# A capped attention with a mixture of experts behind it: tiles' results evacuated within the next tile, x written by units, weights, tables and orders rearranged, chains of tiles unrolled thrice

## The chip, the cores and the metric

The kernel runs on one core of a Trainium2 chip. The time is the device time in microseconds of one execution. Before the change it is 482.37 us, the median of three runs (481.7 to 484.04).

## The reference

Attention runs over 4 batches, 12 heads, 448 tokens and a head size of 64, and its output is the input of a layer with 8 experts, of which each token takes the best one:

```python
scores = scale * (q @ k.T);  scores = cap * tanh(scores / cap)      # cap = 30
attn = exp(scores - max); attn /= sum + 1e-9;  x = attn @ v         # x: 1792 tokens x 768
logits = normed(x) @ normed(expert_emb).T / tau                     # 8 experts
e = argmax(logits);  gate = softmax(logits)[e]
out = gate * (relu(x @ w1[e]) @ w2[e])                              # w1: 768 x 1024, w2: 1024 x 768
```

How many tokens an expert gets is known only while the kernel runs. All is float32, with products to float32 accuracy.

## The kernel before, in words

**Attention** (attention_bounded, L770 to L1013) goes through 12 units of two pairs of heads, three units to a batch. A unit has 7 steps. An iteration of the loop at L942 issues two steps: scores (TensorE: q times k; ScalarE: tanh, then exp) and, four steps behind, values (TensorE: probabilities times v, summed in PSUM buffers v0 and v1). take (L864) lets VectorE divide a pair's sums into xsb, the rows of x in SBUF. embed_v (L826) fills the columns of the next unit's v that a unit needs besides v; it begins with a memset on GpSimd (POOL) at L830. The order of all instructions is as written: each engine runs its own queue in order and waits on semaphores.

**Routing** runs beside it. When a batch is done, after(b) (L895) puts its steps (choose, ranks, norms, scales, gates, each with a cost in us) on the list route, and writes the batch's x to DRAM with write_rows (L437): two transfers, issued by SP, except that columns beyond the first of the last batch are issued by ScalarE. In each iteration the list is served while the planner's sum behind + cost stays at most OVER = 5.2. Weights of the expert that is to run first are loaded into a ring of three pieces, 14 pieces in all, and split into two float16 parts (split_first, L735); fill is the list of the 28 splits, 16 of which are due in the loop. A product of float32 accuracy is three float16 matmuls: high by high, high by low, low by high. first_table (L589), in batch 2, computes the first tiles' row numbers, gathers 128 rows of x from DRAM by them (gather, L216: POOL, an indirect DMA into xg), then runs scale_x (L224: POOL makes x_tile out of xg) and a second gather. later runs transpose_x (L231: TensorE transposes x_tile; ScalarE and VectorE make its two parts) and scale_x six iterations after.

Behind the loop come the first tile's up products, do_up, with the list ready beside them (fills, count_last, what is left of route), the rest of the first tile (tile0) and a branch, `tc.If(unbounded > 0)`, L1140, that goes to a general attention for large caps and is not taken here.

**Experts.** p numbers the experts in the order in which they run. A tile is 128 tokens of one expert (a half tile 64). tile_body (L629) does, in order: gate times scale and the output rows' numbers on POOL (L643 to L657), up products and relu (L258, L270), down products (L675) of six of eight blocks, transpose_x and scale_x for the tile that follows, the last two blocks, then the evacuation by VectorE and ScalarE (L707, L708), the scatter to out (L716) and the gather for a later tile (L721), both on POOL. hooks are put between the blocks: number n before the n-th of 12 up steps and 8 down steps. todo holds the next expert's weight splits (split1, split2), each of which issues the load of the expert after next (load1, load2, through SP). wide_tile (L1384) is the first tile of experts 1 to 4; it carries 32 extra rows (along) with it, which along_gather, along_scale and along_transpose (L1360 to L1375) fetch, scale and transpose once.

Tile 0b (L1536) follows the first tile, with hooks1 (L1301): order (the experts' order), start_loads (SP loads seven registers, then issues expert 1's loads), the last gates, fill_table (all later tiles' row numbers), positions, start_loads2 (w2 of expert 1), along_gather, load_ends (each engine loads how many tiles each expert has). Then chain(p) (L1551) runs an expert's tiles, nested:

```python
with ExitStack() as es:
    for n in range(1, UNROLL):
        es.enter_context(tc.If(code > 2 * n + 1, label=f"more{p}_{n}"))
        full_tile(p, base + n, (), FIRST, {0: [...]})
    es.enter_context(tc.If(code > 2 * UNROLL + 1, label=f"more{p}_{UNROLL}"))
    with tc.For_i(UNROLL, code >> 1, 1) as n:
        full_tile(p, base + n)
```

With this data three full tiles run for p = 0 behind tile 0b, four tiles (one of them wide) for p = 1, three for p = 2, one each for p = 3 and 4, and a half tile for p = 5. More experts (p = 6 and 7, or a second tile of p = 5) run in a branch, "more", that is not taken; expert 6's weights are loaded ahead of it. L1562 is the line of the exits of the nested branches.

## Time and profile before

| | us |
|---|---|
| median of 3 runs | 482.37 (481.7 to 484.04) |
| profiled execution: its time | 480.64 |
| its span | 478.9 |
| busy in the span: PE (TensorE matmul) | 436.3 |
| VectorE (DVE), ScalarE (ACT), GpSimd (POOL) | 273.2, 267.5, 129.0 |
| moved by DMA | 88.21 MB, 184 GB/s on average |

The span is what the profiler records of one execution; the device time of the same execution is 1.7 us more. Attention takes about the first 178 us, the first two tiles until 227, the other tiles until 468; from there to the end no matmul runs. In the rows below, a wait is an engine's idle time and the instruction or transfer that ended it; "issue" is idle time for which the profile shows no cause; a Q behind an engine's name is its instruction queue (sequencer). The granted clock is TensorE's, in parts of 2.4 GHz.

### The profile page before, as it was taken

Reading aid. Unit: us, or ns where it says so; the run is one execution under the profiler, and the core shown is the slowest. Engines: PE = TensorE matmul, PEld = TensorE weight load, DVE = VectorE, ACT = ScalarE, POOL = GpSimd, SP = SyncE. Lnnn points to the kernel's source line nnn. Section 1 sums busy time; section 2 is a strip of 40 time slices with the busy share of each in tenths; the row PEclk is TensorE's granted clock in tenths of the full one; section 3 lists DMA queues with packets and bytes.
Section 4 is the critical chain, followed back from the end, with each engine's and each line's share of the span. In section 5 each row is a group of like instructions: output and inputs, shape, how many; then the busy total and the mean of one; then the engine's idle time right before and its main releaser. Section 6 shows DMA issues by size and latency. Waiting matters only on the chain. (4 is left out here: it accounts for less than half of the span.)

```text
span 478.9 us, 16552 instructions
## 1 busy us (share of the span) xinstructions
PE 436.3 (91%) x7001; PEld 352.6 (74%) x7002; DVE 273.2 (57%) x714; ACT 267.5 (56%) x292; POOL 129.0 (27%) x229
## 2 busy tenths in 40 slices
PE   7999989999996999597969999999999999999771
PEld 3788878888884987394848868878868978869560
DVE  5265577688999589575831139421239321788610
ACT  3999989998999594423720238110248111849200
POOL 5000000000113020213452339322336521573231
PEclk9999999999999899888989999999999999999977
DMA  6844187484288216159972209622219612498940
GB/s 205 298 161 162 54 280 258 156 281 174 78 332 279 73 54 212 58 169 405 403 275 73 71 23 333 236 71 72 71 37 355 250 40 71 135 383 279 380 110 8
DMA packets 29756, 88.21 MB, mean 184 GB/s; under 512 B 6957, under 2 KB 7241, under 8 KB 29650
## 3 DMA queue, kind: packets, MB, share of 16 engines
q1 hardware_dynamic: 26050, 73.31, 42.4%
q0 software_dynamic: 2816, 13.49, 8.7%
q8 instruction: 62, 1.02, 0.9%
q14 instruction: 44, 0.36, 0.2%
q10 hardware_dynamic: 784, 0.03, 0.1%
HBM read 75.10 MB, written 12.31 MB: 183 GB/s over the span
## 5 line engine op out<-in xcount | busy, mean ns | idle before, releaser
L857 PEld LDWEIGHTS v<-vb,prob 128*64 128x64 f32 (+1 forms) x2688 | 80.8, 137 | 21.7 <-issue 15.9
L857 PE MATMUL v<-vb,prob 128*64 128x73 f32 (+1 forms) x2688 | 88.2, 230 | 6.0 <-POOL vb L830 4.0
L258 PEld LDWEIGHTS <-h 128*128 128x128 f16 x1056 | 81.7, 101 | 8.9 <-issue 4.2
L258 PE MATMUL h<-xh,h 128*128 128x128 f16 (+1 forms) x480 | 81.2, 222 | 6.8 <-DMA w2r<-in_moe_w_dram 3.5
L818 ACT ACTIVATE prob<-s,icap 128x896 f32<-128x896 f32 x84 | 80.1, 998 | 12.7 <-PE s L808 11.5
L258 PE MATMUL h<-xl,h 128*128 128x128 f16 (+1 forms) x480 | 81.1, 222 | 1.9 <-issue 1.9
L258 PE MATMUL h<-xh,l 128*128 128x128 f16 (+1 forms) x480 | 81.1, 222 | 0.0
L822 ACT ACTIVATE prob<-prob,cap_b 128x1792 f32<-128x1792 f32 (+1 forms) x47 | 76.8, 1633 | 1.5
L258 PEld LDWEIGHTS <-l 128*128 128x128 f16 x528 | 53.1, 101 | 2.0 <-issue 2.0
L675 PEld LDWEIGHTS <-hh 128*128 128x128 f16 (+1 forms) x352 | 33.3, 101 | 23.2 <-ACT hh L270 3.2
L225 POOL TENSOR_TENSOR x_tile<-xg 128x768 f32<-128x768 f32 x16 | 23.4, 1465 | 97.1 <-PE xt L236 83.6
L270 ACT ACTIVATE hh<-h 128x512 f16<-128x512 f32 (+1 forms) x20 | 11.5, 576 | 67.1 <-PE h L258 62.9
L271 DVE SCALAR_TENSOR_TENSOR hl<-h,hh 128x512 f16<-128x512 f32 (+1 forms) x20 | 13.2, 662 | 62.5 <-ACT hh L270 62.5
L239 ACT CAST xh<-xt 128x384 f16<-128x384 f32 x30 | 12.9, 481 | 56.2 <-PE xt L236 48.6
L1423 PE MATMUL h<-xh,h 128*128 128x160 f16 x192 | 39.9, 233 | 3.4 <-ACTq L1562 3.4
L249 DVE SCALAR_TENSOR_TENSOR l<-w1r,by_pos,h 128x1024 f16<-128x1024 f32 x30 | 36.9, 1281 | 8.2 <-ACT h L248 8.0
L1423 PE MATMUL h<-xh,l 128*128 128x160 f16 x192 | 39.9, 233 | 0.0
L1423 PE MATMUL h<-xl,h 128*128 128x160 f16 x192 | 39.9, 233 | 0.0
L240 DVE TENSOR_TENSOR xl<-xt,xh 128x384 f16<-128x384 f32 x30 | 15.3, 551 | 42.1 <-ACT xh L239 42.1
L675 PE MATMUL y<-h,hl 128*128 128x384 f16 (+1 forms) x160 | 38.9, 334 | 0.0
L675 PE MATMUL y<-l,hh 128*128 128x384 f16 (+1 forms) x160 | 38.8, 333 | 0.0
L675 PE MATMUL y<-h,hh 128*128 128x384 f16 (+1 forms) x160 | 38.6, 331 | 0.0
(292 smaller groups left out, 845.2 us busy)
## 6 DMA issues: line engine op xcount, KB each, us to landing
w1r<-in_moe_w_dram SPq DMA_DIRECT2D x36, 512.0 KB, 6.3
w2r<-in_moe_w_dram SPq DMA_DIRECT2D x24, 768.0 KB, 9.5
qkb<-in_qk_pairs_dram SPq DMA_DIRECT2D x11, 896.0 KB
vb<-in_v_pairs_dram SPq DMA_DIRECT2D x12, 511.0 KB, 7.9
vt<-in_vt_pairs_dram SPq DMA_DIRECT2D x12, 448.0 KB, 6.9
x_dram<-xsb SPq DMA_DIRECT2D x4, 1296.0 KB
ring<-in_moe_w_dram SPq DMA_DIRECT2D x6, 512.0 KB
ring<-in_moe_w_dram SPq DMA_DIRECT2D x8, 384.0 KB
```

Source lines behind the costliest of these rows:

```text
L225: nc.gpsimd.tensor_tensor(x_tile.rearrange("p (h d) -> p h d", d=DH), heads(xg[:, :SCALE]), xg[:, SCALE : SCALE + 1].unsqueeze(2).to_broad ...
L239: nc.scalar.copy(hi, t)
L240: nc.vector.tensor_tensor(lo, t, hi, op=ALU.subtract)
L249: nc.vector.scalar_tensor_tensor(out=lo, in0=raw, scalar=scale, in1=hi, op0=ALU.mult, op1=ALU.subtract, accum_out=acc)
L258: nc.tensor.matmul(hp[:, f, :W], l[j][:, c], x[:, j, :W], start=j == 0 and f == 0 and n == 0, stop=j == DC - 1 and f == 3 and n == 2, skip ...
L270: nc.scalar.activation(b, a, AF.Relu)
L271: nc.vector.scalar_tensor_tensor(out=c, in0=a, scalar=0.0, in1=b, op0=ALU.max, op1=ALU.subtract, accum_out=acc[:, h : h + 1])
L675: nc.tensor.matmul(y, hidden[h][l][:, c, o : o + k], w2p[p % 2][w][f // 2][:, f % 2, m * C : (m + 1) * C], start=f == 0 and n == 0, stop=f ...
L818: nc.scalar.activation(o, sp[:, :, :S], AF.Tanh, scale=icap)
L822: nc.scalar.activation(o, o, AF.Exp, scale=cap_b)
L857: nc.tensor.matmul(psum_v[2 * i + n][h * DH : (h + 1) * DH, m * VW : (m + 1) * VW], pt[rows, s, c : c + DH], vb[rows, k, s, :], start=m == ...
L1423: nc.tensor.matmul(o, w1p[p % 2][l][j][:, c], x[:, j, :], start=j == 0 and f == fs[0] and m == 0, stop=j == DC - 1 and f == fs[-1] and m == 2,
```

## The change

- The two PSUM buffers of the attention's sums become `held`, for the whole kernel. A full or wide tile leaves its result there. hold notes its gate and rows before transpose_x; release, at the start of the next tile, evacuates and scatters. The gather of a tile no longer stands behind its scatter.
- write_rows is called after each unit, for that unit's columns, in place of once per batch.
- first_table only gathers; scale_x and the second gather come three iterations later (first_scale), transpose_x and scale_x behind that. The list route is served to the loop's end; what is left of it, token_rows of the last batch and order come behind the fills, before the first tile's rest.
- Three of the 14 pieces of the first expert's weights go into buffers of q and k (ring_qk) within the last unit.
- Expert 1's w1 loads come behind the first register load. fill_table, positions and start_loads2 move from hook 11 to 9; the copy that start_loads2 waits for moves to POOL, behind a scale_x. along_scale and along_transpose move from hooks 2 and 17 to 12 and 20.
- Expert 6's weights (LATE) are loaded in the "more" branch alone.
- UNROLL is 3.

```diff
-UNROLL = 4
+LATE = WIDE.stop + 1
+UNROLL = 3
...
+    ps_o = ctx.enter_context(tc.tile_pool(name="ps_o", bufs=1, space=PSUM))
+    held = [ps_o.tile([P, 512], F32, tag=f"v{n}", name=f"v{n}") for n in range(2)]
+    held_g = small.tile([P, 1], F32, tag="held_g", name="held_g")
+    held_i = small.tile([P, 1], I32, tag="held_i", name="held_i")
+    def hold(idx, unscaled):
+        nc.gpsimd.tensor_tensor(held_g, gate, unscaled, op=ALU.mult)
+        nc.gpsimd.tensor_copy(held_i, idx)
+    def release():
+        yo = tile_of("o", 0)
+        nc.vector.tensor_scalar(yo[:, :384], held[0][:, :384], held_g, None, op0=ALU.mult)
+        nc.scalar.activation(yo[:, 384:], held[1][:, :384], AF.Copy, scale=held_g)
+        nc.gpsimd.indirect_dma_start(
+            out=out, out_offset=bass.IndirectOffsetOnAxis(ap=held_i[:, :1], axis=0),
+            in_=yo[:], in_offset=None, bounds_check=NT - 1, oob_is_err=False,
+        )
     with ExitStack() as actx:
...
                 nc.tensor.matmul(tp[:, :2], a_all[:, g, :], b0[:, :, g], start=g == 0, stop=g == G3 - 1)
             nc.vector.tensor_scalar(idx0, tp[:, :2], float(NT), None, op0=ALU.add)
             gather(idx0[:, 0:1], EARLY_B * S)
+        def first_scale():
             scale_x()
             gather(idx0[:, 1:2], EARLY_B * S)
...
+            if holds:
+                yb = [t[:, :384] for t in held]
+                if not first:
+                    release()
+            else:
...
                 hook(2 * DC + f)
                 step(pace[2])
                 down(f)
+            if holds:
+                hold(idx, unscaled)
             if nxt is not False:
                 transpose_x()
             if nxt:
             down(7)
             if before:
...
-            for n, (o, w, gt, idx_out, y, yb) in enumerate(parts):
-                yo = tile_of("o", n)
+            if not holds:
+                yo = tile_of("o", 0)
                 C = D // len(yb)
                 if y is None:
                     nc.vector.tensor_scalar(yo[:, :C], yb[0], gt, None, op0=ALU.mult)
...
             if nxt:
                 gather(nxt)
+            hook(2 * DC + FC)
             step(len(todo))
...
         def piece(i):
-            return ring_w[i % 3][:, : F if i < N1 else D]
+            if i < RING:
+                return ring_w[i % 3][:, : F if i < N1 else D]
+            return ring_qk[(i - RING) // 2][:, (i - RING) % 2, :D]
...
-            if h:
+            if h and i + 3 < RING:
                 load_first(e, i + 3)
...
         def count_last():
             rp, c = rank(last), counts(last)
             rank_rows(last, rp)
             tiles(c[:, :E])
-            token_rows(last)
...
                     (0.8, 1, lambda: gates_out(b)),
                 ]
                 if b == EARLY_B - 1:
-                    r.append((0.2, 1, lambda: (first_table(tmp["b"]), later.extend((ROWS_IN, 1)))))
-                write_rows(b, 0, SCALE)
+                    r.append((0.2, 1, lambda: (first_table(tmp["b"]), later.extend([(2, 0, first_scale), (1, 1.2, transpose_x), (2, 0, scale_x)]))))
                 route.extend(r)
...
                         if u == STEPS - 1:
                             take(2 * i + 1)
                             behind += 1.4
-                            if i % (NP // 2) == NP // 2 - 1 and i < NH - 1:
-                                after(i // (NP // 2))
+                            b, n = divmod(i, NP // 2)
+                            write_rows(b, 4 * n * HW, 4 * (n + 1) * HW)
+                            if n == NP // 2 - 1 and b < last:
+                                after(b)
...
+                        if i == NH - 1 and u in (1, 5):
+                            for n in (0, 1) if u == 1 else (2,):
+                                load_first(pre["e"], RING + n)
...
                     if later:
-                        later[0] -= 1
-                        if later[0] <= 0 and len(later) > 1:
-                            later.pop()
-                            transpose_x()
-                            scale_x()
-                            behind += 1.2
-                    while 8 <= g0 < last_step and route and since >= route[0][1] and behind + route[0][0] <= OVER:
+                        wait, cost, f = later[0]
+                        if wait:
+                            later[0] = wait - 1, cost, f
+                        else:
+                            later.pop(0)
+                            f()
+                            behind += cost
+                    while 8 <= g0 and route and since >= route[0][1] and behind + route[0][0] <= OVER:
...
                     left = len(fill) - len(FIRST_SPLITS) + IN_TIME
-                    if g0 >= last_step - 2 or left > 0 and (behind < 3.9 or 2 * left >= last_step - g0):
+                    if g0 >= last_step and not route or left > 0 and (behind < 3.9 or 2 * left >= last_step - g0):
                         do_fill()
                         behind += 1.25 if len(fill) > len(FIRST_SPLITS) - 12 else 1.0
                     behind = max(0.0, behind - ROOM)
-                write_rows(last, 0, SCALE)
...
                     0: [do_fill], 1: [do_fill, square[0]], 2: square[1:2], 5: square[2:3],
-                    7: [count_last, *[f for _, _, f in route], do_fill, do_fill],
+                    7: [count_last, do_fill, do_fill],
                     8: [square[3], lambda: norms_x(last)], 9: [do_fill], 10: [do_fill],
...
-                yp = [ps_o.tile([P, 512], F32, tag=f"v{n}", name=f"yp{n}") for n in range(2)]
+                for _, _, f in route:
+                    f()
+                token_rows(last)
+                order()
                 tc.mark_branch_hint_location("any", unbounded > 0, engines=TOLD)
-                tile0(lambda n, i: yp[i][:, :384] if n == "y" else x_tile)
+                tile_body(0, idx0[:, 0:1], None, hidden=first_h, first=True)
...
-    def load1(p, i):
-        if p < E:
+    def load1(p, i, late=False):
+        if p < E and (late or p != LATE):
             nc.sync.dma_start(raw1[i], w1_part(eid[p], i))
...
         gather(col(start))
         scale_x()
+        nc.gpsimd.tensor_copy(pos_l, pos_e[:, 1:2])
         gather(col(start + 1))
...
-        for i in range(N1):
-            load1(1, i)
+            if p == 1:
+                for i in range(N1):
+                    load1(1, i)
     def start_loads2():
-        nc.vector.tensor_copy(pos_l, pos_e[:, 1:2])
         e = nc.values_load(pos_l, engines=(ET.SP,), min_val=0, max_val=E - 1)
...
     hooks1 = {
         0: [
-            order, start_loads, lambda: scales_x(last), lambda: gates(last), lambda: gates_e(last),
+            start_loads, lambda: scales_x(last), lambda: gates(last), lambda: gates_e(last),
             lambda: gates_out(last), slots,
         ],
-        11: [lambda: fill_table(start), positions, start_loads2],
+        9: [lambda: fill_table(start), positions, start_loads2],
         13: [lambda: along_gather()],
         **{15 + n: [lambda i=i: load_ends(i) for i in range(3 * n, min(3 * n + 3, E))] for n in range(3)},
...
-        g = small.tile([P, 1], F32, tag="gt0", name="gt0", bufs=2)
-        idx_out = small.tile([P, 1], I32, tag="idx_out0", name="idx_out0", bufs=3)
-        nc.gpsimd.tensor_tensor(g, gate, unscaled, op=ALU.mult)
-        nc.gpsimd.tensor_copy(idx_out, col(base))
+        release()
...
+        hold(col(base), unscaled)
         transpose_x()
         scale_x()
...
-        yo = tile_of("o", 0)
-        nc.vector.tensor_scalar(yo[:, :384], y[0], g, None, op0=ALU.mult)
-        nc.scalar.activation(yo[:, 384:], y[1], AF.Copy, scale=g)
-        nc.gpsimd.indirect_dma_start(
-            out=out, out_offset=bass.IndirectOffsetOnAxis(ap=idx_out[:, :1], axis=0),
-            in_=yo[:], in_offset=None, bounds_check=NT - 1, oob_is_err=False,
-        )
         gather(col(base + 3))
         step(len(todo))
...
     def full_tile(p, slot, *args, **kw):
-        any_tile(p, slot, slot + 3, P, *args, **kw)
+        any_tile(p, slot, slot + 3, P, *args, holds=p < WIDE.stop, **kw)
...
                 if not p:
-                    hooks |= {2: [along_scale], 2 * DC + 5: [along_transpose, lambda: along_behind(1)]}
+                    hooks |= {2 * DC: [along_scale], 2 * DC + FC: [along_transpose, lambda: along_behind(1)]}
                 full_tile(p, base, todo_for(p + 1), FIRST if p else FIRST0, hooks)
...
         position(1)
+        release()
...
         with tc.If(more > 0, label="more"):
+            for i in range(N1):
+                load1(LATE, i, True)
+            for f in range(N2):
+                load2(LATE, f, True)
```

## Rows read from the trace of the kernel before

**Rows 1.** The page: span, and busy time of each engine

```profile
span 478.9 us, 16552 instructions
PE 436.3 (91%) x7001; PEld 352.6 (74%) x7002; DVE 273.2 (57%) x714; ACT 267.5 (56%) x292; POOL 129.0 (27%) x229
```

**Rows 2.** What PE waited for: us in total, times, longest us

```profile
PE v L857 <- POOL vb L830: 4.0, 1, 4.0
PE along_t L1372 <- POOL room L1361: 4.0, 1, 4.0
PE xt L236 <- POOL x_tile L225: 3.5, 1, 3.5
PE h L258 <- DMA w2r<-in_moe_w_dram: 3.5, 1, 3.5
PE h L1423 <- ACTq L1562: 3.4, 4, 1.1
PE h L258 <- ACTq L1140: 3.3, 1, 3.3
PE yp L675 <- ACT hh L270: 2.8, 1, 2.8
PE h L258 <- issue: 1.9, 1, 1.9
```

**Rows 3.** Stretches: us, busy PE, PEld, DVE, ACT, POOL, granted clock, DMA share, GB/s

```profile
155.65:159.15 3.50, 3.50 (x60) 3.50 (x62) 0.05 (x2) 0.00 (x0) 0.09 (x1) 0.52 0.49 131
305.00:321.00 16.00, 16.00 (x197) 13.12 (x196) 3.20 (x8) 2.63 (x5) 4.29 (x8) 1.00 0.26 90
355.40:360.00 4.60, 4.60 (x67) 4.60 (x68) 3.15 (x5) 4.33 (x5) 3.76 (x3) 1.00 0.37 124
455.75:462.40 6.65, 4.74 (x90) 4.64 (x91) 0.00 (x1) 0.38 (x1) 3.08 (x4) 0.52 0.31 101
462.40:468.30 5.90, 5.90 (x107) 4.47 (x104) 1.79 (x8) 0.38 (x1) 0.56 (x4) 0.96 0.42 69
```

**Rows 4.** Timeline of POOL, batch 3: start us, length us, engine, line, operation

```profile
142.70 1.27 POOL L219 DMA_INDIRECT xg<-x_dram,idx_in  x1 [1.13 <-issue]
151.54 1.46 POOL L225 TENSOR_TENSOR x_tile<-xg 128x768 f32<-128x768 f32 x1 [7.57 <-DMA xg<-x_dram,idx_in]
```

**Rows 5.** Tile xg: from a gather's issue to its landing

```profile
DMA to landing us min/median/max: 4.1/5.7/8.8
```

**Rows 6.** Timeline of ACT, then of DVE, around the first tiles

```profile
190.01 0.23 ACT L465 ACTIVATE ex<-lg 128x32 f32<-128x32 f32 x1 [5.90 <-DVE lg L462]
203.09 0.16 DVE L1535 TENSOR_TENSOR sums<-sums,acc 128x2 f32<-128x2 f32 x1 [2.73 <-DVEq L1140]
```

**Rows 7.** Timeline of POOL in tile 0b

```profile
214.17 1.06 POOL L219 DMA_INDIRECT xg<-x_dram,idx_in  x1 [0.99 <-DMA w1r<-in_moe_w_dram]
221.22 1.46 POOL L225 TENSOR_TENSOR x_tile<-xg 128x768 f32<-128x768 f32 x1 [5.99 <-DMA xg<-x_dram,idx_in]
```

**Rows 8.** Timeline of POOL behind tile 0b

```profile
233.43 0.18 POOL L241 COPY gates<-gates 128x1 f32<-128x1 f32 x1 [7.02 <-issue]
```

**Rows 9.** Timeline of DVE at the end

```profile
469.05 0.62 DVE L714 TENSOR_SCALAR yo<-y,gt 128x384 f32<-128x384 f32 x1 [2.71 <-POOL gt L657]
```

**Rows 10.** Timeline of POOL, then of PE, at the end of p=1's third tile

```profile
336.26 1.47 POOL L225 TENSOR_TENSOR x_tile<-xg 128x768 f32<-128x768 f32 x1 [10.20 <-PE xt L236]
337.96 0.22 PE L258 MATMUL h<-xh,h 128*128 128x128 f16 x1
```

**Rows 11.** What SP's queue waited for

```profile
SPq L439 <- DVE xsb L879: 17.3, 3, 15.0
```

**Rows 12.** Line 439, ScalarE's part: count, min/median/max ns

```profile
L439 ACTq DMA_DIRECT2D x_dram<-xsb x1: 627/627/627, 206.3 to 206.3; - x1
```

**Rows 13.** Timeline of DVE, then of ACT, at unit 10's last take

```profile
172.17 0.59 DVE L879 TENSOR_SCALAR xsb<-v,inv 64x72 f32<-64x72 f32 x2
172.48 0.99 ACT L818 ACTIVATE prob<-s,icap 128x896 f32<-128x896 f32 x1
```

More of the change, by code (lines that the diff above doesn't have):

```diff
@@ L758, in attention_moe, with order @@
         last = B - 1
+        pos_e = small.tile([1, E], I32, tag="pos_e", name="pos_e")
+        perm = small.tile([P, E, E], F32, tag="perm", name="perm")
+        def order():
+            nc.vector.tensor_tensor(
+                perm,
+                iota_t[:, :E].unsqueeze(2).to_broadcast([P, E, E]),
+                place.unsqueeze(1).to_broadcast([P, E, E]),
+                op=ALU.is_equal,
+            )
+            which = small.tile([1, E, E], F32, tag="which_e", name="which_e")
+            nc.vector.tensor_tensor(which, perm[0:1], iota_t[0:1, :E].unsqueeze(1).to_broadcast([1, E, E]), op=ALU.mult)
+            with nc.allow_low_precision("numbers of experts, exact"):
+                nc.vector.tensor_reduce(pos_e, which, axis=AX.X, op=ALU.add)
         def count_last():
@@ L1110, in attention_any @@
                 e = first_register()
+                for n in range(3):
+                    load_first(e, RING + n)
                 for i, h in FIRST_SPLITS:
@@ L1120, in attention_any @@
                     relu(h, hp, acc0, tiles=first_h[h])
-                yp = [pz.tile([P, 512], F32, tag=f"z{2 * n + 1}", name=f"yp{n}") for n in range(2)]
                 choose(last)
@@ L1124, in attention_any @@
                 count_last()
-                tile0(lambda n, i: yp[i][:, :384] if n == "y" else x_tile)
+                token_rows(last)
+                order()
+                tile_body(0, idx0[:, 0:1], None, hidden=first_h, first=True)
         nc.scalar.dma_start(emb_sb, emb)
@@ L1182, in split2 @@
         load2(p + 1, f)
-    def order():
-        nc.vector.tensor_tensor(
-            perm,
-            iota_t[:, :E].unsqueeze(2).to_broadcast([P, E, E]),
-            place.unsqueeze(1).to_broadcast([P, E, E]),
-            op=ALU.is_equal,
-        )
-        which = work.tile([1, E, E], F32, tag="which_e", name="which_e")
-        nc.vector.tensor_tensor(which, perm[0:1], iota_t[0:1, :E].unsqueeze(1).to_broadcast([1, E, E]), op=ALU.mult)
-        with nc.allow_low_precision("numbers of experts, exact"):
-            nc.vector.tensor_reduce(pos_e, which, axis=AX.X, op=ALU.add)
     def slots():
@@ L1442, in wide_tile @@
         nc.vector.tensor_tensor(sum_h, sum_h, acc, op=ALU.add)
-        y = [tile_of("y", n) for n in range(2)]
+        y = [t[:, :384] for t in held]
         passes = ((0, 0), (0, 1), (1, 0))
@@ L1547, in half_tile @@
         def half_tile(p, hooks=(), before=None):
[L1549 removed]
+            any_tile(p, ends[p][1], False, P // 2, hooks=hooks, before=before, holds=False)
         def chain(p):
```

72 lines of the change are left out of this document (30 added, 42 removed).

## The prediction

> **What bounds the kernel now.** I read the page first: TensorE (PE) is busy 436.3 us of a 478.9 us span, 91% [rows 1]. More overlap can win at most the idle rest, so the second view was what PE waited for [rows 2]. It lists eight causes above 1.5 us. Six are single waits of 2.8 to 4.0 us; the seventh is four crossings into the next expert's code (3.4 us in four, the longest 1.1); the eighth is 1.9 us of instruction supply. Together they are 26.4 us. The third view, PE's clock by stretch [rows 3], adds what the waits cost behind themselves. After the 4.0 us wait the granted clock is 0.52 over 3.5 us, so 3.5 x 0.48 = 1.7 us of work comes late: the 1.2 GHz level for nearly all of that stretch. After the 0.76 us crossing at 355.38 it stays 1.00. So I charge a wait of 3 to 4 us some 1.7 us (1.5 below 3) on top of its length, a crossing nothing more. In the steady tiles the clock is 1.00 and PE is busy 16.00 of 16.00 us [rows 3]; there the change can win nothing.
>
> The span ends with a chain: the last half tile, its result, its scatter. So waits anywhere on PE and all of the tail count fully.
>
> **The change part by part** (gains negative, bounds in brackets, against the profiled execution's 480.64 us).
>
> *A, embed_v's wait (4.02).* POOL issues first_table's gather at 142.70, then scale_x stands in its queue until 151.54 (7.57 us of waiting for the landing), a second gather follows [rows 4], and only then the memset of vb, for which PE stands [rows 2]. Now scale_x and the second gather come three iterations later. An iteration is two steps of about 2.2 us each (84 steps in some 190 us), so 13 us, more than the 8.8 that any gather took to land [rows 5]. The memset then finds POOL free: 4.02 + 1.68 = -5.7 [-4.0 to -6.1; ScalarE, idle behind this wait too, may hand a little back or more].
>
> *B, the first relu (2.81).* ScalarE waited 5.90 us for VectorE's lg, since token_rows, count_last and the route's rest all stood before it [rows 6]; then fills, then the relu. The change puts the route's rest, token_rows and order behind the fills. The wait is worth 2.81 plus 1.5 of clock. But fewer fills are done within the loop's last iterations, so fills move here; and the same VectorE work now stands before the branch at L1140. I take -3.5 [-0.5 to -4.5].
>
> *C, the branch at L1140 (3.31).* VectorE reaches tile 0b's code with 2.73 us of crossing in its own queue [rows 6], so the price is mostly the crossing. The evacuations and their scatter go behind it (1.2 us), the moved route work before it: -1.0 [0 to -3].
>
> *D, x_tile (3.54).* The gather is issued at 214.17 (the row names a w1r load before it; by the code it waits for the gate writes to x), and lands 7.05 us later, at 221.22 [rows 7], in a stretch that the w1 and w2 loads fill. fill_table moves from hook 11 to 9 but the gates' write still bounds it; w2's loads now wait for a POOL copy behind the gather's landing, so it runs with less traffic and should take near the shortest 4.1 to the median 5.7 [rows 5]. Of 3.54 plus some 1.7 of clock, 5.2, I take -2.8 [0 to -5.2].
>
> *E, along_t (3.99).* POOL reaches load_ends' end at 233.43 after 7.02 us in register loads; everything behind runs late [rows 8], along_scale, for which PE stands, last of all. along_transpose moves from hook 17 to the tile's end, three weight blocks and the transposes later, about 3.6 us, and the scatter no longer stands before the gather. Of 3.99 + 1.7 = 5.7 I take -4.7 [-1 to -5.7]; the cover is this POOL backlog staying below 3.6 us.
>
> *F, crossings.* ScalarE came last at the four [rows 2], since it evacuated the tile first; that is now behind the crossing. PE's own crossing remains: -0.9 over three [0 to -1.5]; the fourth is in H.
>
> *G, the last half tile.* It waits 3.53 us for w2 [rows 2], as ring traffic of expert 6 (LATE) is in front of it; those loads are gone unless the extra branch is taken. Left is a crossing of 0.76: -2.8. From 455.75 to 462.40 the clock was 0.52 [rows 3], of which 1.9 is idle: 4.7 us of work at half speed, 2.4 lost, of which I keep 2.1 won. Sum -4.9 [-3.5 to -8]. Behind it, VectorE's evacuation started at 469.05, after 2.71 us of waiting for POOL's gt [rows 9], while PE was done at 468.3 [rows 3]; gt comes in POOL's queue behind two scatters and a gather now, and one scatter fewer then. PE's end to the evacuation, 0.75, becomes 0.2: -0.55 [0 to -1].
>
> *H, unrolled thrice.* Expert p=1 has four tiles, so its fourth runs in the loop, once. No row shows a loop. Its exit makes every engine wait for what is under way, PE for the gather too, which that tile issues last. At the end of its third tile scale_x ran from 336.26 for 1.47 us, and the next tile's first matmul was at 337.96 [rows 10]. Without the scatter ahead, the gather would be issued some 0.6 us after scale_x, at PE's end plus 0.4, and land 4.1 to 8.8 later, median 5.7 [rows 5]. Against the 0.76 paid today PE idles 3.7 to 8.4 us more, by the median 5.3; with the clock's 1.7 this is 5.4 to 10.1. This tile runs in quiet traffic, so I take near the shorter end, +6.5 [+2, should the exit not wait for it in full, to +11, with extra instruction supply].
>
> The Trainium skill, "DMA: Bandwidth & Descriptors", section "Anatomy of one DMA", fits such a transfer with 2.0 us plus bytes over 436 GB/s; for 128 rows of 866 words, 443 KB, that gives an estimate of 3.0 us, and H would be +3.8, the time 463.6. The trace's shortest is 4.1 [rows 5], so the rows decide. Its "Runtime: NRT & Kernel Launch", section "Instruction fetch mechanics", says that a taken branch out of the prefetched window stalls on a fetch; at the crossings the trace shows 0.76 without one and 1.9 us of supply once [rows 2]; by the rule the loop would cost 1.9 more, 468.2.
>
> *I, x written by units.* Each of the 12 units issues two writes, 24 for 8. Those of three batches stay on SP: 0, since SP stood 17.3 us in three waits for such a write's data, the longest 15.0 [rows 11], and no PE wait names the loads queued behind. But of the last batch write_rows puts columns beyond the first on ScalarE's queue, so four issues of 0.63 us [rows 12] move there. Unit 10's two stand before the last two softmax steps, on the engine that sets that stage's pace, and wait for VectorE's take, which ended at 172.76, 0.3 us after ScalarE was free for those steps [rows 13]: 2 x 0.63 + 0.3 = +1.5. Unit 11's fall into the wait for lg. I take +1.5 [-1 to +4].
>
> *Nothing counted for:* hold's two POOL operations (0.2 us each, in a tile of 16.5 where POOL is busy 4.3 [rows 3]); the moved evacuations, same length, beside the next tile's first matmuls; the ring pieces loaded early, 3 of 14, on a queue that has waits of many us [rows 11].
>
> Sum: -5.7 -3.5 -1.0 -2.8 -4.7 -0.9 -4.9 -0.55 +6.5 +1.5 = -16.05, that is 464.6 for the profiled execution. The median shown, 482.37, is 0.36% above 480.64, so 466.3.
>
> **The rivals.** *R2, the loop costs nothing* (its exit doesn't hold PE, or the landing is hidden): 466.3 - 6.5 = 459.8. For it: no row shows the wait. Against: the exit waits on all engines, and gathers never landed below 4.1.
> *R3, waits only move.* VectorE carries fills and route work up to the branch, POOL its backlog to along_t: B, D and E, 11.0 us, are not won: 477.3. For it: VectorE was the last at lg, and POOL took 7.02 us for the register loads, which stay [rows 6, 8].
> *R4, slower: SP's queue.* Eight of the twelve units, those that end no batch, newly put two writes into a queue, seven of them into SP's, that wait for VectorE's take; the head loads queued behind come late, or ScalarE does, and embed_v and scores stall PE each time. One such stall costs A's 5.7; eight cost 45.6, against -16 a time of 512. It decides from 16 / 8 = 2.0 us per unit. Against it: the 15.0 us wait went by unnoticed [rows 11], and head loads are issued a unit ahead.
> That a part doesn't do what it says lies inside these: in C and F the crossing may be PE's own, and 1.9 us less is won.
>
> **How the numbers follow.** My forecast, 466.3 (own range 460 to 472), 0.55; R2 0.18; R3 0.22; R4 0.05. A difference of 0.5% (2.4 us) is about what a measurement can tell from no change. R1 and R2 are faster wholly, R3 nearly so (by its bounds it may reach the band around 482.4), R4 slower: faster 0.93, same 0.03, slower 0.04. For 8 in 10 the range takes R1, nearly all of R2 and the better half of R3: 457 to 477.
>
> **What would show it.** Right: no PE wait for vb; the half tile's w2r wait gone; one new PE idle of about 5 us before the second wide tile, behind the loop, with the clock at half after it; x_tile's and along_t's waits below 2.5 us. Wrong: the relu's wait replaced by one on VectorE before L1140; PE waiting in attention for qkb, vb or their splits (R4); no gap behind the loop (R2).

## The result, and the profile after

The changed kernel takes 489.49 us, the median of four runs (487.63 to 490.94), the kernel before 483.01 in the same four-run comparison. The ratio is 1.0133, 95% interval 1.0087 to 1.018: slower by 1.3%, where 466.3 (457 to 477) was forecast. The profiled execution took 490.94 us, 10.3 more than that of before, while the medians lie 6.5 apart; stretches below are read against the 10.3.

The page's first rows of after, against [rows 1]: PE's work is the same in number, and the span has grown around it.

```profile
span 489.2 us, 16614 instructions
PE 439.9 (90%) x7001; PEld 354.5 (72%) x7002; DVE 274.4 (56%) x713; ACT 267.1 (55%) x292; POOL 131.0 (27%) x230
```

What PE waited for in after, against [rows 2]. The wait for vb and the one that names w2r are gone, but as many others stand there:

```profile
PE h L1448 <- PEq L1581: 6.9, 3, 5.1
PE h L1448 <- issue: 6.4, 2, 5.6
PE xt L236 <- POOL x_tile L225: 5.4, 1, 5.4
PE h L258 <- DVEq L1182: 4.6, 1, 4.6
PE h L258 <- DVE yo L308: 3.8, 1, 3.8
PE v L692 <- ACT hh L270: 3.3, 1, 3.3
PE v L889 <- issue: 3.2, 3, 1.4
PE v L692 <- DVE hl L271: 1.5, 2, 1.2
```

The first matmuls of the tiles cut both traces into the same stretches (us, first matmul to first matmul):

| stretch of before | before | after | difference | forecast |
|---|---|---|---|---|
| to the first tile's up products | 178.5 | 176.1 | -2.4 | A, I: -4.2 |
| to tile 0b (203.10) | 24.6 | 23.2 | -1.5 | B, C: -4.5 |
| tile 0b (to 226.85) | 23.8 | 26.0 | +2.2 | D: -2.8 |
| p=0's first full tile (to 250.10) | 23.3 | 24.8 | +1.6 | E: -4.7 |
| to p=1's fourth tile (337.96) | 87.9 | 87.9 | 0.0 | F: -0.3 |
| that tile, loop in after (to 355.38) | 17.4 | 22.3 | +4.9 | H: +6.5 with the next row |
| p=2 (to 409.91) | 54.5 | 56.2 | +1.7 | F: -0.3 |
| p=3's wide tile (to 431.45) | 21.5 | 26.0 | +4.5 | F: -0.3 |
| p=4's, and the half tile, to PE's end | 36.8 | 36.8 | 0.0 | G: -4.9 |
| PE's end to the span's end | 10.6 | 10.0 | -0.7 | -0.55 |

Three places have to be explained here: tile 0b, the tile behind it and the exit of expert 3. The loop's exit is compared with H behind them; the last half tile, where G's gain is missing, is taken up where the prediction is judged.

*Tile 0b.* SP's issues, ScalarE's two gate writes and POOL's gather, in after's timeline (start, length, engine; the answer to [rows 7]):

```profile
200.40 3.08 SPq L1207 DMA_DIRECT2D w1r<-in_moe_w_dram  x6
```

```profile
202.53 0.57 ACTq L456 DMA_DIRECT2D x_dram<-xsb  x1
203.13 0.85 ACTq L459 DMA_DIRECT2D x_dram<-xsb  x1
```

```profile
208.26 0.22 POOL L218 COPY idx_in<-table 128x1 int32 x1 [6.14 <-issue]
215.37 1.06 POOL L219 DMA_INDIRECT xg<-x_dram,idx_in  x1 [6.89 <-DMA w1r<-in_moe_w_dram]
219.67 1.46 POOL L225 TENSOR_TENSOR x_tile<-xg 128x768 f32<-128x768 f32 x1 [3.24 <-DMA xg<-x_dram,idx_in]
```

The row numbers are ready at 208.26, but the gather goes out at 215.37: it waits, by the code for the gate writes (the view names a w1r load). These were issued at 202.53 and 203.13, after 3 MB of w1 loads that the change issues from 200.40 on. From tile 0b's first matmul to the gather it is 16.1 us; before it was 11.1.

*The tile behind it* (p=0's first full tile). POOL, ScalarE twice, PE:

```profile
231.85 0.19 POOL L303 TENSOR_TENSOR held_g<-gates,first_u 128x1 f32<-128x1 f32 x1 [6.86 <-issue]
232.07 0.58 ACT L309 ACTIVATE yo<-v,held_g 128x384 f32<-128x384 f32 x1 [8.77 <-POOL held_g L303]
236.10 0.58 ACT L270 ACTIVATE hh<-h 128x512 f16<-128x512 f32 x1
236.73 0.50 PE L692 MATMUL v<-h,hh 128*128 128x384 f16 x2 [3.31 <-ACT hh L270]
```

hold's multiplication stands behind 6.86 us of register loads on POOL. ScalarE waits 8.77 us for its result, as its evacuation is now the first thing in the new tile, so its weight splits and then its relu come late, and PE waits for the relu. In the other traces that hold behind the down products this tile takes 21.7 to 24.1 us, so the 24.8 of after is the upper end.

*The exit of expert 3.* PE's, POOL's queue entries at L1581 (count, min/median/max ns, first and last start), then ScalarE and PE:

```profile
L1581 PEldq COMPARE_BRANCH  x1: 7067/7067/7067, 434.9 to 434.9; - x1
L1581 POOLq INC_SWDGE_SEM  x1: 841/841/841, 439.8 to 439.8; - x1
L1581 PEldq EVENT_SEMAPHORE  x1: 51/51/51, 442.1 to 442.1; - x1
```

```profile
442.26 0.58 ACT L309 ACTIVATE yo<-v,held_g 128x384 f32<-128x384 f32 x1 [8.59 <-PEq L1581]
442.44 0.28 PE L1448 MATMUL h<-xh,h 128*128 128x160 f16 x1 [5.14 <-PEq L1581]
```

PE's branch begins at 434.9 and takes 7.07 us; its matmuls ran out at 437.3. (PEldq is PE's queue in this view.)

*The loop's exit.* POOL's gather, PE, and then the clock by stretch (columns as in [rows 3]):

```profile
354.68 1.08 POOL L219 DMA_INDIRECT xg<-x_dram,idx_in  x1 [0.27 <-POOL idx_in L218]
360.20 0.29 PE L1448 MATMUL h<-xh,h 128*128 128x160 f16 x1 [5.64 <-issue]
```

```profile
354.60:360.20 5.60, 0.00 (x1) 0.04 (x2) 0.05 (x1) 0.37 (x1) 1.08 (x1) 0.73 0.29 84
360.20:363.70 3.50, 3.50 (x27) 3.50 (x28) 2.78 (x4) 3.50 (x5) 2.03 (x1) 0.50 0.00 0
```

This is H as forecast: the gather goes out near PE's end, PE stands for 5.6 us, and the clock is 0.50 for the 3.5 us behind. The mechanism shows too: at the loop's line (L1588) the queues of PE, ScalarE, VectorE and POOL all stand until 358.7, and the gather landed at 358.63; the rest, 1.5 us, is the engines' way out of the loop.

```profile
L1588 PEldq EVENT_SEMAPHORE  x9: 51/51/6302, 352.4 to 359.6; - x9
```

### The profile page after: what moved, and what is told of

It reads as the page before. It is cut to its first block, busy times and chain, and to the rows that moved or that the text cites. A ratio compares the mean times of both kernels' runs of the same rounds, so it can differ in the third digit from the quotient of the medians.

```text
span 489.2 us, 16614 instructions
## 1 busy us (share of the span) xinstructions
PE 439.9 (90%) x7001; PEld 354.5 (72%) x7002; DVE 274.4 (56%) x713; ACT 267.1 (55%) x292; POOL 131.0 (27%) x230
## 3 DMA queue, kind: packets, MB, share of 16 engines
q8 instruction: 63, 1.03, 0.9%
## 5 line engine op out<-in xcount | busy, mean ns | idle before, releaser
L258 PEld LDWEIGHTS <-h 128*128 128x128 f16 x1056 | 81.0, 100 | 10.2 <-issue 9.2
L1448 PE MATMUL h<-xh,h 128*128 128x160 f16 x192 | 42.2, 242 | 12.6 <-PEq L1581 6.9
L692 PEld LDWEIGHTS <-hh 128*128 128x128 f16 (+1 forms) x352 | 33.4, 101 | 24.5 <-ACT hh L270 3.5
L225 POOL TENSOR_TENSOR x_tile<-xg 128x768 f32<-128x768 f32 x16 | 24.1, 1503 | 85.5 <-PE xt L236 72.4
L692 PE MATMUL v<-h,hh 128*128 128x384 f16 (+1 forms) x176 | 43.2, 335 | 3.3 <-ACT hh L270 3.3
L1448 PEld LDWEIGHTS <-h 128*128 128x128 f16 x384 | 33.8, 102 | 15.1 <-issue 8.6
L692 PE MATMUL v<-h,hl 128*128 128x384 f16 (+1 forms) x176 | 42.9, 333 | 1.5 <-DVE hl L271 1.5
L692 PE MATMUL v<-l,hh 128*128 128x384 f16 (+1 forms) x176 | 43.6, 335 | 0.6 <-DVE l L249 0.5
L1448 PE MATMUL h<-xl,h 128*128 128x160 f16 x192 | 42.1, 242 | 0.8 <-issue 0.8
L1448 PE MATMUL h<-xh,l 128*128 128x160 f16 x192 | 42.1, 242 | 0.0
```

Of the source, the lines that this page charges most:

```text
L225: nc.gpsimd.tensor_tensor(x_tile.rearrange("p (h d) -> p h d", d=DH), heads(xg[:, :SCALE]), xg[:, SCALE : SCALE + 1].unsqueeze(2).to_broad ...
L258: nc.tensor.matmul(hp[:, f, :W], l[j][:, c], x[:, j, :W], start=j == 0 and f == 0 and n == 0, stop=j == DC - 1 and f == 3 and n == 2, skip ...
L692: nc.tensor.matmul(y, hidden[h][l][:, c, :W], w2p[p % 2][w][f // 2][:, f % 2, m * C : (m + 1) * C], start=f == 0 and n == 0, stop=f == FC ...
L1448: nc.tensor.matmul(o, w1p[p % 2][l][j][:, c], x[:, j, :], start=j == 0 and f == fs[0] and m == 0, stop=j == DC - 1 and f == fs[-1] and m == 2,
```

## The experiments

All times are against runs of the kernel before on the same chip (medians 481.6 to 482.4); the ratio's 95% interval follows the time.

**The change undone one part at a time.** e1 is `-UNROLL = 3` / `+UNROLL = 4`.

> The changed kernel with UNROLL = 4 again; nothing else differs. Theory H (the loop's exit holds every engine until the gather under way has landed, and the half clock follows): the gap of 5.64 us before 360.20 becomes a crossing of about 0.8, the second wide tile runs at full clock, and the time is 6.5 us lower than the changed kernel's 489.5, about 483. Rival (the loop's exit isn't the cause, the gap is an instruction fetch that moves with the code): a gap of several us stays at p=1's end or moves to another expert's end, and the time is within 2.5 us of 489.5.

481.76 us, ratio 1.0002 (0.9973 to 1.0031). The loop's gap is gone. So is the gap at expert 3's exit, which was not expected:

```profile
PE xt L236 <- POOL x_tile L225: 5.1, 1, 5.1
PE h L1448 <- PEq L1581: 1.8, 3, 0.7
```

e2 takes expert 1's w1 loads back behind all register loads:

```diff
-            if p == 1:
-                for i in range(N1):
-                    load1(1, i)
+        for i in range(N1):
+            load1(1, i)
```

> The changed kernel with expert 1's w1 loads issued behind all seven register loads, as before the change. Theory D (the gate writes on ScalarE's queue land late because 3 MB of w1 loads were issued 2 us ahead of them; the first gather waits for them): the gather goes out some 11 us after tile 0b's first matmul instead of 16, PE's 5.44 us wait for x_tile shrinks below 2, and the time is 3 to 5 us lower, 484.5 to 486.5. Rival (the gather waits for something else, or lands as much later as it is issued earlier beside the loads): the wait for x_tile stays above 4 us and the time within 1.5 us of 489.5.

487.11 us, 1.011 (1.007 to 1.0149). POOL's timeline there shows the gather out 10.9 us after tile 0b's first matmul (199.33), and the wait for x_tile is 2.2 us (theory D had below 2). Tile 0b takes 23.8 us instead of 26.0. Theory D holds in its mechanism; the size is 2.2, not 3 to 5, as the gather now lands beside the loads, in 6.7 us instead of 4.3.

```profile
210.22 1.06 POOL L219 DMA_INDIRECT xg<-x_dram,idx_in  x1 [0.95 <-DMA w1r<-in_moe_w_dram]
216.93 1.80 POOL L225 TENSOR_TENSOR x_tile<-xg 128x768 f32<-128x768 f32 x1 [5.64 <-DMA xg<-x_dram,idx_in]
```

e3 puts `hold(idx, unscaled)` ahead of tile_body's down products.

> The changed kernel, but tile_body notes a tile's gate and rows (hold) ahead of its down products instead of behind six of them. Theory E (in tile 0b hold's two operations stand on POOL behind 7 us of register loads, ScalarE and VectorE wait 8.8 and 8.2 us for held_g at the head of the next tile, and its relu and PE wait for them): these two waits and PE's waits of 3.31 and 1.18 us go, and the time is 4 to 6 us lower, 483.5 to 485.5. Rival (ScalarE's queue of splits is late by itself): PE still waits 3 us or more for the relu and the time stays within 1.5 us of 489.5.

487.37 us, 1.0131 (1.009 to 1.0172): by the time alone nothing. In the trace the stretch of p=0's first full tile is 19.8 us instead of 24.8, the relu's waits are gone, and 2.1 us of along_t's are back. The stretch speaks for theory E; the runs' spread of 4 us doesn't let the time confirm it.

```profile
PE along_t L1400 <- POOL room L1389: 2.1, 1, 2.1
```

e4 writes x once per batch: `write_rows(b, 0, SCALE)` if n is the batch's last unit.

> The changed kernel with each batch's x written once, behind its third unit, as before the change. Theory I (two more writes of each unit in SP's queue wait for VectorE's take, the head loads behind them come late, and the attention loses 3.2 us between its 8th and its 44th step): the 44th step comes about 3 us earlier, at 93.5, the attention ends 2 to 4 us earlier, and the time is 485.5 to 487.5. Rival (the 3.2 us come from elsewhere, such as the loads' own traffic): the 44th step stays at 96.6 and the time within 1.5 us of 489.5.

485.73 us, 1.0101 (1.0057 to 1.0145). The 44th step comes at 92.3. But attention moves from run to run: over all traces that have first_table split, the first tile's up products start at 175.5 on average in eight with unit writes (174.2 to 176.8) and 173.7 in six without (171.8 to 176.2). With the attention of the kernel before they start at 178.5 (before), 182.5 (e5) and 184.8 (e6), although its code is the same in these three. So I is some 1.8 us, from averages whose single traces differ by more, and not this run's 4.3. About half of it lies before the 44th step (from the 8th to the 44th 69.6 us on average with unit writes, 68.8 without), where only SP writes.

**Parts alone, in the kernel before.** e5 is the kernel before with UNROLL = 3.

> The kernel before with UNROLL = 3, nothing else. In the runs so far the changed kernel with four unrolled tiles is 7.7 us faster than with three: 5 to 6 us are the gap at the loop's exit, and 4 to 5 a slow PE branch at expert 3's exit. Theory (both belong to the three tiles, whatever else the kernel does): PE idles 5 us or more before the second wide tile and 4 us or more before the fourth, and the time is 6 to 12 us above the kernel before, 488 to 494. Rival (the exit waits for the gather only because the change issues it late in the tile without the scatter, or the slow branch comes from the code's other lengths): one of the two gaps is missing, and the time is 0 to 5 us above, 482 to 487.

500.51 us, 1.035 (1.0274 to 1.0427). Beyond either expectation:

```profile
PE h L1423 <- POOL idx_out L1393: 8.6, 1, 8.6
PE h L1423 <- PEq L1562: 3.8, 1, 3.8
```

Without the change's earlier gather the loop's exit costs 8.6 us, and PE's branches out of experts 3 and 4 take 5.8 and 5.5 us. Three tiles everywhere are dear in both kernels. (4 us of the profiled execution's excess lie in its attention, which the edit doesn't touch.)

e6 leaves expert 6's loads to the extra branch (`if p < E and (late or p != 6)`, and the loads in the branch).

> The kernel before, with expert 6's weights loaded in the extra branch alone. Theory G as predicted (the half tile waits for w2 behind these loads): PE's 3.53 us wait before 455.75 goes, most of the half clock behind it too, and the time is 4 to 5.5 us lower, 477 to 478.5. Rival (the wait is PE's branch out of expert 4's tile, 4.6 us long in that trace, whose fetch the loads only lengthen): a gap of 1.5 us or more stays there, and the time is 0 to 3 us lower, 479.5 to 482.5.

478.95 us, 0.9954 (0.9912 to 0.9995). PE's wait ahead of the half tile falls from 3.53 to 1.3 us, the other from 1.9 to 1.4:

```profile
PE h L258 <- issue: 1.4, 1, 1.4
PE h L258 <- ACTq L1562: 1.3, 1, 1.3
```

The stretch to PE's end is 32.0 us instead of 36.8, so G's -4.9 was right for this kernel, by the trace; the time falls between the two expectations, and its interval reaches from 0 to -4. And both causes had a share: PE's branch there took 4.60 us in before and 2.21 without the loads. The row that named w2r [rows 2] hid a branch that the loads lengthened.

e7 is first_table split alone, as in the change.

> The kernel before with first_table split alone: the gather there, scale_x and the second gather three iterations later. Theory A: PE's 4.02 us wait for the memset of vb goes, 5.6 us with the clock, no new wait appears, and the time is 4.5 to 6 us lower, 476.5 to 478. Rival (the later transposes or scale_x stall the attention or the first tile's up products instead): a new wait of 1.5 us or more between 150 and 185 us, and the time is 0 to 3 us lower.

476.61 us, 0.9869 (0.9812 to 0.9926). No wait for vb, no new one: theory A holds.

**Together.** e8 is the changed kernel with the edits of e1 to e4.

> The changed kernel with four unrolled tiles, expert 1's loads behind the register loads, hold ahead of the down products, and each batch's x written once. If what the four runs showed one by one adds up (7.7, 2.4, 2.1 and 3.8 us from 489.5), the time is 473 to 475. Rival (the gains share one stretch, since the first two meet in tile 0b and its successor): 477 to 480.

474.54 us, 0.9831 (0.9777 to 0.9884). Against the changed kernel that is 15 us less; the four alone, against its 489.49, give 7.7, 2.4, 2.1 and 3.8, together 16. Within the spread of these runs the times add up. The traces don't quite: tile 0b and the tile behind it take 50.8 us together in the changed kernel, 46.9 with e2's edit, 46.1 with e3's and 45.6 with both, so there the gains are shared, as the rival says; in e8 PE waits 3.9 us for along_t again. (The execution of e8 that was profiled took 479.35 us, the longest of six.)

**Expert 3's exit.** e9 and e10 unroll four tiles for one expert alone (`unroll = 4 if p == 1 else UNROLL`, and 3 in place of 1).

> The changed kernel (489.5) with four tiles unrolled for expert 1 alone, three for the others: no loop runs any more, but expert 3's exit jumps over the same code as in the changed kernel. Theory (the slow PE branch at expert 3's exit comes from the three-tile code of that expert, and its fetch): the 5.64 us gap before the second wide tile becomes 0.7, the gap of 4 to 5 us before the fourth stays, and the time is 482.5 to 484.5. Rival (the branch is slow because a loop ran before): both gaps go, 480 to 482, as with four tiles everywhere (481.8).

> The changed kernel with four tiles unrolled for expert 3 alone: the loop runs for expert 1 as in the changed kernel. Theory (three-tile code of expert 3): the 5.6 us gap at the loop's exit stays, the gap before the fourth wide tile goes below 1 us, and the time is 483 to 485.5. Rival (a loop ran before): the gap before the fourth wide tile stays at 4 us or more, and the time within 1.5 us of 489.5.

e9: 472.39 us, 0.9793 (0.9757 to 0.9828); e10: 484.48, 1.0057 (1.0034 to 1.008). Neither theory survives the traces, though e10's time lies in the first one's range. In e9 no loop runs and PE's branch still takes 4.65 us (a 2.6 us gap); in e10 expert 3 has four tiles and it takes 6.38. e9 is 9 us faster than four tiles everywhere, which no theory here had.

**The kernel before with what gained.** e11 is e6 and e7 together; e12 adds the change's hooks (9, 12 and 20), with results evacuated in their own tile.

> The kernel before with the two parts that gained alone, first_table split and expert 6's loads left to the extra branch (5.0 and 2.6 us). If they add up, since they lie 300 us apart: 473.5 to 475 by the kernel before's 481.6 to 482.4. Rival (one of the two gains was chance): 476 or more.

471.46 us, 0.9808 (0.9757 to 0.9859): below the expected span, but its interval holds the sum.

> The kernel of the run above (first_table split, expert 6's loads later) with the change's hooks besides: fill_table, positions and start_loads2 at 9, along_scale at 12, along_transpose at the tile's end; results leave PSUM within their own tile, as before. Theory E without hold and release (along_transpose has 3.6 us more of cover): PE's wait for along_t falls from 4.2 below 1 us and the time is 3 to 5 us under that run's, 469 to 471.5. Rival (POOL is later by as much, or another wait takes the place): along_t or another of PE's waits there stays above 3 us, and the time within 1.5 us of that run's.

466.49 us, 0.9679 (0.9619 to 0.9739). p=0's first full tile takes 18.4 us (before: 23.3), 4.9 less: E's -4.7, without hold.

```profile
PE along_t L1377 <- POOL room L1366: 1.0, 1, 1.0
PE xt L236 <- POOL x_tile L225: 2.6, 1, 2.6
```

**Results held or not.** e13 takes the held results out of the combined kernel:

```diff
-            any_tile(p, slot, slot + 3, P, *args, holds=p < WIDE.stop, **kw)
+            any_tile(p, slot, slot + 3, P, *args, holds=False, **kw)
...
-        tile_body(0, idx0[:, 1:2], col(start + 2), hooks=hooks1)
+        release()
+        tile_body(0, idx0[:, 1:2], col(start + 2), hooks=hooks1, holds=False)
```

A wide tile there evacuates and scatters at its own end, as in the kernel before; only the first tile's results are still held, up to tile 0b. The edits of e1, e2 and e4 are in it, that of e3 has nothing left to act on.

> The combined kernel (four tiles, expert 1's loads behind the register loads, each batch's x written once) with results evacuated within their own tile, as before the change; the first tile's alone is still held. Theory (held results cost, since at the head of the next expert's tile ScalarE and VectorE must wait until POOL has come through the crossing, and the splits and relus queue behind them): no wait of ScalarE or VectorE for an evacuation above 4 us, no PE wait for a relu in the wide tiles, and the time is 464 to 468, 6 us or more under the combined kernel's 474.5. Rival (held results are free, and the faster kernels owe their time to the attention): 472.5 to 476.5.

464.58 us, 0.9654 (0.9622 to 0.9686): the fastest here, 3.5% under the kernel before, 10 us under e8 (8.5 by the two ratios). PE's branches out of experts 3 and 4 are no shorter than in e8 (1.7 and 1.9 us against 1.9 and 0.4), so they don't explain it. At expert 4's entry in e8, the queues of PE and POOL, then ScalarE:

```profile
L1581 PEldq EVENT_SEMAPHORE  x1: 51/51/51, 425.9 to 425.9; - x1
L1581 POOLq COMPARE_BRANCH  x1: 64/64/64, 426.4 to 426.4; - x1
L1581 POOLq INC_SWDGE_SEM  x1: 810/810/810, 432.9 to 432.9; - x1
```

```profile
433.82 0.58 ACT L309 ACTIVATE yo<-v,held_g 128x384 f32<-128x384 f32 x1 [11.51 <-DMA out_dram<-yo,held_i]
```

PE was done at 425.9. ScalarE, idle since 422.3, evacuates at 433.82, 0.1 us after POOL has come through the crossing (432.9 plus 0.81). In after the last to cross is PE (442.1), and ScalarE starts at 442.26. In e13 the same evacuation comes ahead of the crossing:

```profile
418.26 0.58 ACT L1509 ACTIVATE yo<-v,gt 128x384 f32<-128x384 f32 x1 [3.62 <-PEq L1591]
```

So a result that is held over the end of an expert is evacuated when the last of POOL and PE has crossed, and splits and relus of the next tile wait in the queue behind it. Expert 4's wide tile takes 30.2 us in e8 and 22.1 in e13, p=0's first full tile 24.5 and 18.8. The label that the view gives to ScalarE's wait (a scatter, landed at 430.47) can't be the cause alone; the moment fits POOL's last entry.

What POOL's crossing takes depends on the chain's length, which no expectation had. Out of experts 3 and 4, from POOL's branch to the end of its INC_SWDGE_SEM, it takes 6.6 to 7.7 us (11.0 and 11.2 once each) at all 19 exits of an expert with four unrolled tiles, and 1.6 to 1.7 at all 15 with three. So the 8 us in expert 4's tile are a price of held results and four tiles together. In the changed kernel, with three, POOL is through at 440.61 and the evacuation (442.26) comes with PE's first matmul (442.44). In e9 experts 3 and 4 have three tiles and no loop runs: expert 4's tile takes 22.1 us and the half tile's matmuls 8.5, against 29.2 and 13.5 in e1. These two are 12 us less, more than the 9 by which e9 is the faster.

**The place of the code.** e14 and e15 repeat six up products in the branch for large caps, which isn't taken: 144 PE instructions more, none of them run.

> The changed kernel with 72 more matmuls and 72 weight loads in the branch for large caps, which is not taken: nothing more runs, but PE's code behind the attention lies 144 instructions further on. If the place of the code sets the time of PE's branch at expert 3's exit, this branch (5 to 7 us in five traces of three-tile kernels) takes 2 us or less, or moves to another exit, and the time changes by 3 us or more from 489.5. If three tiles set it in another way, it stays at 5 to 7 us and the time within 2 us of 489.5. The loop's exit keeps its 5.6 us gap by either.

> The same 144 instructions that never run, in the changed kernel with four unrolled tiles (481.8). If the place of the code sets the branch's time, PE's branch at expert 3's or expert 4's exit (0.4 and 1.7 us there) takes 3 us or more in this one or the one above changes, and the time moves by 2 us or more. If not, both stay below 2 us and the time within 2 us of 481.8.

e14: 479.65 us, 0.9958 (0.9928 to 0.9989), ten below the changed kernel. e15: 482.07, 0.9995 (0.996 to 1.003), as e1. PE's branches out of experts 3 and 4: of e1, then e14, then e15:

```profile
L1581 PEldq COMPARE_BRANCH  x1: 473/473/473, 425.2 to 425.2; - x1
L1581 PEldq COMPARE_BRANCH  x1: 1687/1687/1687, 453.4 to 453.4; - x1
```

```profile
L1584 PEldq COMPARE_BRANCH  x1: 4307/4307/4307, 431.5 to 431.5; - x1
L1584 PEldq COMPARE_BRANCH  x1: 345/345/345, 454.8 to 454.8; - x1
```

```profile
L1584 PEldq COMPARE_BRANCH  x1: 4407/4407/4407, 425.5 to 425.5; - x1
L1584 PEldq COMPARE_BRANCH  x1: 3383/3383/3383, 455.0 to 455.0; - x1
```

With three tiles the branch at expert 3's exit falls from 7.07 to 4.31 us and the one at expert 4's from 2.85 to 0.35; with four they rise from 0.47 to 4.41 and from 1.69 to 3.38. Instructions that never run move both, so the place of the code is a cause. e14's fall is less than the "2 us or less" expected, and e15's total doesn't show its rise.

The traces show what the branch waits for. Of the DMA queues that carry instructions, q8 moved 1.03 of 1.36 MB in after, in packets of 16 KB; as PE and its weight loads are 14,003 of 16,614 instructions, I take it for PE's code. The page of after has the first line below. The second is the view of the DMA queues from 439.4 to 440.4, inside the branch of 7.07 us; from 434.9 to 439.4 there is no such packet.

```profile
q8 instruction: 63, 1.03, 0.9%
q8 instruction: 1, 0.02, 5.9%
```

Behind 250 us the 17 traces have 37 PE branches of 1.0 us or more. Each ends 1.3 to 1.7 us after a packet of q8 has landed; the 37 between 0.3 and 0.4 us have none so near. In the 13 branches above 3.3 us the packet begins only 1.0 to 4.6 us behind the branch. What delays it is shown for expert 4's exit alone: where expert 6's loads run, it begins 2.1 (before) and 2.8 us (e7) behind the branch, and without them 0.3 to 0.5 us ahead of it (e6, e11, e12, e13).

## Why the prediction was wrong

A (-5.7) was right (e7), H (+6.5) too: +4.9 and +1.7 in the trace (the 7.7 by which e1 is faster hold expert 3's exit too). I had the size (+1.8 for +1.5), in part by luck: about half of it lies in the stretch where the prediction had SP's writes at 0. Between the forecast (-16.05) and the profiled execution (+10.3) lie 26.3 us: E lacks 6.3, D 5.0, G 4.9, F 4.8 at expert 3's exit, B and C 3.0; the rest is small. No single step turns the sign. These failed:

- **"Nothing counted for: hold's two POOL operations [...]; the moved evacuations, same length, beside the next tile's first matmuls."** The operations are short, but they stand behind POOL's register loads, and the evacuations stand at the head of ScalarE's and VectorE's queues, behind a crossing. It ate E: that tile takes 24.8 us with hold behind the down products, 19.8 with hold ahead of them (e3; 24.5 in e8, behind a shorter tile 0b) and 18.4 and 18.8 without held results (e12, e13). With four tiles and e8's other edits, results that aren't held are worth 10 us more (e13 against e8); no run takes them out of the changed kernel with its three tiles.
- **G, "those loads are gone [...] Left is a crossing of 0.76".** The price held in the kernel before (e6), though the wait that names w2r was for its larger part PE's branch, which the loads lengthened. In after another wait of 3.79 us stands ahead of the half tile's first matmul, which the prediction didn't have:

```profile
467.76 0.62 DVE L308 TENSOR_SCALAR yo<-v,held_g 128x384 f32<-128x384 f32 x1 [3.70 <-DMA out_dram<-yo_a,idx_a]
469.38 0.20 PE L258 MATMUL h<-xh,h 128*128 128x64 f16 x1 [3.79 <-DVE yo L308]
```

The view names the release, but the matmul comes 1.0 us behind its end, and it doesn't need it: in e14 it comes 2.2 us ahead of the release, in e1 and e8 6 us and more.

```profile
458.63 0.19 PE L258 MATMUL h<-xh,h 128*128 128x64 f16 x1 [1.36 <-issue]
460.78 0.62 DVE L308 TENSOR_SCALAR yo<-v,held_g 128x384 f32<-128x384 f32 x1 [3.70 <-DMA out_dram<-yo_a,idx_a]
```

What lies in after's 3.79 us is the end of PE's branch (2.85 us from 463.14) and, behind PE's last queue entry at 467.3, a packet of q8 that lands at 467.96, 1.4 us ahead of the matmul. So by these times G's gain went to PE's code; no run isolates it.

- **D, "the gates' write still bounds it".** Right as a rule, but the loads issued ahead of the write were counted only as traffic beside the gather. They delay the gather, by the code through the write (e2): +2.2 instead of -2.8; 5.0 off, of which e2 gives back 2.2.
- **F, "PE's own crossing remains: -0.9".** The crossings stayed at 1.1 and 0.7, and at expert 3's exit PE's branch took 7 us, and the stretch grew by 4.5, which no step had. That branch's time changes with code that never runs (7.07 to 4.31 us in e14). The Trainium skill, "Runtime: NRT & Kernel Launch", section "Instruction fetch mechanics", says that a taken branch to a target outside the fetched pages stalls on a fetch; the prediction weighed it for the loop alone. The traces agree: the branch of 7.07 us ends 1.5 us after a packet of the instruction queue q8 has landed.
- **B and C, -4.5.** The relu's wait of 2.81 went; the crossing became 4.6 us where it was 3.3, which fits the moved VectorE work, R3's "VectorE carries [...] route work up to the branch" (no run takes that work back). -1.5.

A reading was short besides: the view behind [rows 2] has a ninth cause above 1.5 us, 2.0 us of issue at L857, so PE's listed waits are 28.4 us and not 26.4. No term rests on it.

R3 had the mechanism of B and E, but in the wrong place for E; it was priced as gains that don't come, at 477.3, not as losses. R4 had SP's queue; the unit writes cost some 1.8 us in all. No rival held both that edits would cost in places where nothing was charged and that waits of 7 us could appear at branches that were fast.

Open: why the packet of PE's code comes late at one exit and not at another, and why POOL's crossing is long with four tiles. With three tiles everywhere PE's branch at expert 3's exit was slow in all six traces (4.3 to 7.1 us), but with four tiles at that expert it was slow in e10 and e15 as well (6.38 and 4.41). A slow branch of PE need not cost its length: e9's at expert 3's exit is longer than e1's (4.65 against 0.47), and e9 is 9 us faster; e1 and e15 lose 7 us in expert 4's tile, where ScalarE and VectorE evacuate late.

## What to carry to other kernels

Before moving a result's evacuation over a control-flow boundary, name the engine that crosses last, and what stands in the evacuating engine's queue behind it. A transfer that unblocks others (here a small write of gates) is better issued ahead of bulk loads: in e2 the gather went out 5 us earlier, and 2.2 us were left of it. When unrolled code changes its length, look at each branch's own duration on PE's queue, and repeat the measurement with the code shifted before a gain or loss of 2% is put down to the edit.

## What the runs showed of the hardware

144 instructions that never run changed the time by 10 us in one kernel (489.5 to 479.7) and by nothing in another (481.8 to 482.1). PE's branch took from 0.47 to 7.07 us out of expert 3 and from 0.35 to 5.47 out of expert 4; all 37 branches of 1.0 us or more end 1.3 to 1.7 us after a 16 KB packet of the instruction queue q8 has landed. POOL's crossing there took 6.6 us or more with four unrolled tiles and 1.6 to 1.7 with three. A loop's exit held every engine until the gather under way had landed (358.63; PE idle for 5.6 us). A DMA named as the end of a wait [rows 2] can be the last thing that landed while the branch was the cause: 4.60 us for the branch before the half tile, against the 3.53 of that row.

```profile
L1562 PEldq COMPARE_BRANCH  x1: 4601/4601/4601, 449.8 to 449.8; - x1
```
